# Linear attention ahead of two MLPs on one core: k and v on 128 partitions with a shared last chunk, and a softmax in pieces on ScalarE

## The chip, the core and the metric

One core of a Trainium2 chip. The time is that of one execution on the device in microseconds (us); less is better.

## What is computed

```python
q_s = exp(q - max(q, axis=-1)); q_s = q_s / (sum(q_s, axis=-1) + 1e-09)
k_s = exp(k - max(k, axis=2));  k_s = k_s / (sum(k_s, axis=2) + 1e-09)
kv  = einsum('bhsd,bhse->bhde', k_s, v)      # 4 batches, 8 heads, 576 rows, 64 wide
x   = einsum('bhsd,bhde->bhse', q_s, kv)     # then as 2304 tokens of 512
h   = x @ w_in1;  x   = (h / (1 + exp(-1.702 * h))) @ w_out1    # 512 -> 2048 -> 512
h   = x @ w_in2;  out = (h * tanh(log1p(exp(h)))) @ w_out2      # 512 -> 2048 -> 512
```

The softmax of k subtracts the largest value of each column (batch, head, d) over the sequence. All data is fp32.

## The kernel before

The 2304 tokens are six blocks of 384. For each block the attention makes x (`attention`, L705), and the first MLP runs over 16 chunks of its inner width (`gemm_in`, L750, with `gelu`, and `gemm_out`, L790). The second MLP follows for all blocks (`gemm_in2`, L875, and `gemm_out2`, L918). The MLPs' matmuls are split: each fp32 operand is a sum of two fp32r parts, and three of the four products are taken, so that three matmuls of 384 columns stand for one. The weights are loaded raw and put into the two parts by three to five operations on ScalarE and VectorE (`weight`, L366); those of the first MLP during the first block and the second block's attention, in which the attention's work competes with them.

A unit `u` is a batch and a pair of heads: 16 units, four per batch. Batch 0 belongs to block 0, batch 1 to block 1 (which straddles two batches), batches 2 and 3 to blocks 3 and 4. The 576 rows of the sequence lie as 96 partitions (`KP`) by 6 chunks (`KC`, L245). Per unit:

- `k_load` and `v_load` (L423, L433) fetch a pair of heads. k is one DMA; v is one DMA into a dense tile and a copy on ScalarE in block 0, and one DMA per head later. The tiles of v have two more columns of ones, which give the sums.
- `k_max` (L467) takes the maximum over the chunks on VectorE (three operations, L476), transposes it on TensorE (L481) and reduces it over the partitions (L482).
- In batches 0 and 1 `k_first` (L484) subtracts it on TensorE in plain fp32: an identity matmul of k and one of `minus` by the maxima into the same bank, 384 columns each, for each head (L494, L497), then the exponential out of PSUM (L510). In batches 2 and 3 `k_later` (L516) turns the maxima back (L520), subtracts them on VectorE (L522) and takes the exponential (L523).
- `k_kv` (L525) multiplies: for each head six accumulated matmuls of one chunk, 64 columns of weights and 66 moving columns (L533). The second head writes the other 64 partitions of the same bank. Then the division by the sum (L545 to L565).

An fp32 matmul is two records of the profile, each with its own weight load.

The softmax of q (`q_soft`, L593) works on half a block, four heads: [128, 12, 64] in one tile. VectorE takes the maximum (L611), VectorE or GpSimd subtracts it (`either`, L329), ScalarE takes the exponential of all 768 columns (L613), VectorE sums (L614), adds 1e-9 (L615), inverts (L616) and multiplies (L329). `q_turn` and `x_part` (L633, L664) transpose q and multiply by kv.

The order of all instructions on all engines is made by a planner (`Plan`, L20): each operation is handed in with an engine (or two to choose from), a cost in ns, and what it reads and writes; a list scheduler walks forth and back six times and emits the best order. SyncE issues all DMAs in that order (`dma`, L318, with at least 650 ns each for the planner). The costs are the author's numbers; a different cost gives another order.

Of the kernel before, what the change touches and what calls it, by code (L numbers as in the profile page):

```python
# [8 lines left out]
F32 = mybir.dt.float32  # L9
# [201 lines left out]
def tile_attention_moe_moe(  # L211
# [21 lines left out]

    nc = tc.nc
    P = 128
# [9 lines left out]
    KC = 6  # L245
    KP = S // KC
# [3 lines left out]
    ND = 3  # L250
    SPLIT = ((0, 0), (0, 1), (1, 0))
# [26 lines left out]
    kt = [ap.tile([KP, 2, KC, D], F32, name=f"kt{i}") for i in range(2)]  # L278
    vt = [ap.tile([KP, 2, KC, D + 2], F32, name="vt0")]
    qt = ap.tile([P, NCT, 4, D], F32, name="qt")  # L280
    kv = [ap.tile([P, 2, P], F32R, name=f"kv{i}") for i in range(NHP)]
    pmt = [ap.tile([KP, P], F32, name=f"pmt{i}") for i in range(NHP)]
# [3 lines left out]
    kx = [ap.tile([KP, 2, 3, D], F32, name=f"kx{i}") for i in range(2)]  # L286
    rs = ap.tile([P, NHP], F32, name="rs")
    qs = ap.tile([P, 2, 12], F32, name="qs")

# [3 lines left out]
    kt += [sp.tile([KP, 2, KC, D], F32, name=f"kt{i}") for i in range(2, NHP)]  # L293
    vt += [sp.tile([KP, 2, KC, D + 2], F32, name=f"vt{i}") for i in range(1, NHP)]
    vr = [sp.tile([KP, 2, KC * D], F32, name=f"vr{i}") for i in range(2)] + [gt2[0:KP]]
# [5 lines left out]
    for t in vt:  # L301
        nc.gpsimd.memset(t[:, :, :, D : D + 2], 1.0)
# [15 lines left out]
    def dma(size, reads, writes, out, in_, slow=1):  # L318
        plan.op(
            [(DMA, max(size * slow / 280.0, 650.0), lambda: nc.sync.dma_start(out=out(), in_=in_()), False)],  # L320
            reads,
            writes,
        )
# [93 lines left out]
    def k_tile(u):  # L417
        return u if u < NHP else u % 2

    def v_tile(u):  # L420
        return u if u < NHP else 0

    def k_load(u):  # L423
        b, hp = divmod(u, NHP)
        dma(
            S * 512,
            [],
            [("kt", k_tile(u))],
            lambda: kt[k_tile(u)],
            lambda: k[b, 2 * hp : 2 * hp + 2].rearrange("h (p c) d -> p h c d", c=KC),  # L430
        )

    def v_load(u):  # L433
        b, hp = divmod(u, NHP)
        key = ("vt", v_tile(u))
        if b == 0:

            dense, dk = vr[hp % 3], [("vr", hp % 3)] if hp % 3 < 2 else [("gt", 0), ("gt", 1)]
            dma(
                S * 512,  # L440
                [],
                dk,
                lambda: dense,
                lambda: v[b, 2 * hp : 2 * hp + 2].rearrange("h (p c) d -> p h (c d)", c=KC),
            )
            to = vt[v_tile(u)][:, :, :, 0:D]
            of = dense.rearrange("p j (c d) -> p j c d", d=D)
            plan.op(
                [
                    (ACT, act_ns(768), lambda: nc.scalar.activation(out=to, in_=of, func=AF.Copy), False),  # L450
                    (POOL, 1200.0, lambda: nc.gpsimd.tensor_copy(out=to, in_=of), True),
                ],
                dk,
                [key + (j,) for j in range(2)],
            )
            return
        for j in range(2):
            dma(
                S * 256,
                [],  # L460
                [key + (j,)],
                lambda j=j: vt[v_tile(u)][:, j, :, 0:D],
                lambda j=j: v[b, 2 * hp + j].rearrange("(p c) d -> p c d", c=KC),
                slow=2,
            )

    def k_max(u, ps, key):  # L467

        kk = ("kt", k_tile(u))
# [4 lines left out]
        xk = ("kx", u % 2)  # L474
        largest = lambda n, out, in0, in1, reads, writes: dve(
            n, reads, writes, lambda: nc.vector.tensor_tensor(out=out, in0=in0, in1=in1, op=ALU.max), pair=True  # L476
        )
        largest(384, x, t[:, :, 0:3], t[:, :, 3:6], [kk], [xk])
        largest(128, wide, x[:, :, 0], x[:, :, 1], [xk], [pk])
        largest(128, wide, wide, x[:, :, 2], [xk, pk], [pk])  # L480
        pe(110, [pk], [key], lambda: nc.tensor.transpose(ps, pm, ident[0:KP, 0:KP]))  # L481
        dve(96, [key], [mk], lambda: nc.vector.reduce_max(out=m, in_=ps, axis=AX.X))  # L482

    def k_first(u, ps, keys):  # L484


        kk, mk = ("kt", k_tile(u)), ("mc", u % NHP)
        t, m = kt[k_tile(u)], mcol[:, u % NHP : u % NHP + 1]
        k_max(u, ps[0][:, NB : NB + KP], keys[0])
        for j in range(2):  # L490

            def less(j=j):
                o = ps[j][0:KP, 0:NB]
                nc.tensor.matmul(  # L494
                    out=o, lhsT=ident[0:KP, 0:KP], rhs=t[:, j].rearrange("p c d -> p (c d)"), start=True, stop=False
                )
                nc.tensor.matmul(  # L497
                    out=o.rearrange("p (c d) -> p c d", d=D),
                    lhsT=m.to_broadcast([P, KP]),
                    rhs=minus[:, j * D : (j + 1) * D].rearrange("p (o d) -> p o d", o=1).to_broadcast([P, KC, D]),  # L500
                    start=False,
                    stop=True,
                )

            pe(1330, [("kt", k_tile(u)), ("kt", k_tile(u), j), mk], [keys[j]], less, whole=True)
            act(
                NB,
                [keys[j]],
                [("kt", k_tile(u), j)],
                lambda j=j: nc.scalar.activation(  # L510
                    out=t[:, j].rearrange("p c d -> p (c d)"), in_=ps[j][0:KP, 0:NB], func=AF.Exp
                ),
                psum=True,
            )

    def k_later(u, ps1, ps2, key):  # L516
        kk, mk = ("kt", k_tile(u)), ("mc", u % NHP)
        t, m = kt[k_tile(u)], mcol[:, u % NHP : u % NHP + 1]
        k_max(u, ps1[:, 0:KP], key)
        pe(110, [mk], [key], lambda: nc.tensor.transpose(ps2[0:KP, :], m.to_broadcast([P, KP]), ident))  # L520
        far = ps2[0:KP, :].rearrange("p (j o d) -> p j o d", j=2, o=1).to_broadcast([KP, 2, KC, D])
        dve(768, [kk, key], [kk], lambda: nc.vector.tensor_tensor(out=t, in0=t, in1=far, op=ALU.subtract))  # L522
        act(768, [kk], [kk], lambda: nc.scalar.activation(out=t, in_=t, func=AF.Exp))  # L523

    def k_kv(u, ps3, key3):  # L525
        kk = ("kt", k_tile(u))
# [13 lines left out]

        pe(1375, [kk] + [("kt", k_tile(u), j) for j in range(2)] + [("vt", v_tile(u), j) for j in range(2)], [key3], mm, whole=True)
# [51 lines left out]
    def q_soft(blk, half):  # L593
# [369 lines left out]
    def idle():  # L963
# [9 lines left out]
        + [("kt", i) for i in range(2, NHP)]  # L973
        + [("vt", i, j) for i in range(1, NHP) for j in range(2)]
        + [("vr", i) for i in range(2)]
        + [("qr", i) for i in range(2)],
# [9 lines left out]
    for n in range(NS):  # L986
# [14 lines left out]
        if n == NS - NFC:  # L1001
            plan.op(
                [(NONE, 0.0, pool_second, False)],
                [],
                [("second",)]
                + [("kt", i) for i in range(2)]
                + [("vt", 0, j) for j in range(2)]
                + [("qt", j, d) for j in range(4) for d in (0, 192)]
                + [("kv", hp, a, j) for hp in range(NHP) for a in range(2) for j in range(2)]
                + [("kv32", hp, j) for hp in range(NHP) for j in range(2)]  # L1010
                + [(s, i) for s in ("qT32", "kx") for i in range(2)]
                + [("pm", i) for i in range(NHP)]
                + [(s, i) for s in ("mc", "rs") for i in range(NHP)]
                + [("qs", i) for i in range(2)],
            )
# [54 lines left out]
```

## Time and profile before

| | |
|---|---|
| median of 3 runs | 892.26 us (891.75 to 892.71) |
| the profiled execution | 892.4 us, its span 890.6 us |
| TensorE busy | 880.1 us (99%) |
| VectorE busy | 395.7 us (44%) |
| ScalarE busy | 361.6 us (41%) |
| granted TensorE clock, mean | 0.998 of 2.4 GHz |

The span runs from the first instruction to the last. Busy times of TensorE overlap in the records, since matmuls are pipelined: a record lasts longer than the step to the next one's start, and the step is what a matmul costs. The first 121 us hold block 0 and the attention of block 1, 230 to 345 us the attention of blocks 3 and 4, and from 484 us the second MLP runs.

### The profile page before, as it was taken

Reading aid. Unit: us, or ns where it says so; the run is one execution under the profiler, and the core shown is the slowest. Engines: PE = TensorE matmul, PEld = TensorE weight load, DVE = VectorE, ACT = ScalarE, POOL = GpSimd, SP = SyncE. Lnnn points to the kernel's source line nnn. Section 1 sums busy time; section 2 is a strip of 40 time slices with the busy share of each in tenths; the row PEclk is TensorE's granted clock in tenths of the full one; section 3 lists DMA queues with packets and bytes.
Section 4 is the critical chain, followed back from the end, with each engine's and each line's share of the span. In section 5 each row is a group of like instructions: output and inputs, shape, how many; then the busy total and the mean of one; then the engine's idle time right before and its main releaser. Section 6 shows DMA issues by size and latency. Waiting matters only on the chain.

```text
span 890.6 us, 12257 instructions
## 1 busy us (share of the span) xinstructions
PE 880.1 (99%) x4961; PEld 819.4 (92%) x4961; DVE 395.7 (44%) x760; ACT 361.6 (41%) x649; POOL 5.3 (1%) x21
## 2 busy tenths in 40 slices
PE   8999999999999999999999999999999999999998
PEld 5797899999999999999999999899899899899897
DVE  7999993263385276226999911101101101101101
ACT  5987873242353244224778821311321321321321
POOL 1000000000000000000000000000000000000000
PEclk9999999999999999999999999999999999999999
DMA  9676762011132021100355302001001001000001
GB/s 249 202 224 181 202 208 72 1 36 71 27 90 99 1 71 45 59 1 18 118 167 187 120 1 71 36 1 71 36 1 71 36 1 71 36 1 0 36 1 36
DMA packets 63145, 65.80 MB, mean 74 GB/s; under 512 B 32497, under 2 KB 54513, under 8 KB 62577
## 3 DMA queue, kind: packets, MB, share of 16 engines
q1 hardware_dynamic: 63088, 65.02, 24.2%
q8 instruction: 39, 0.64, 0.3%
q14 instruction: 18, 0.14, 0.0%
HBM read 54.00 MB, written 11.01 MB: 73 GB/s over the span
## 4 chain that ended last, share of the span: by engine, by line
PE 90%; DVE 5%; ACT 2%; DMA 2%; issue 1%; SPq 0%; DVEq 0%
PE hp L755 23%; PE acc L929 22%; PE acc L796 20%; PE h L755 20%; PE at L533 1%; DVE dec L393 1%; DVE dec L398 1%; DMA raw<-in_moe_w_in_dram 1%; PE at L667 1%; PE at L638 1%; DVE W L329 1%; PE at L676 1%; DMA raw<-in_moe_w_out_dram 1%; DVE gt L773 1%; DVE g L329 0%
## 5 line engine op out<-in xcount | busy, mean ns | idle before, releaser
L755 PE MATMUL h<-xt,W 128*128 128x384 f32 x1152 | 224.0, 339 | 1.0 <-DVE gt L773 0.8
L796 PE MATMUL acc<-g,W 128*128 128x384 f32 x1152 | 223.2, 339 | 0.1
L755 PE MATMUL hp<-xt,W 128*128 128x384 f32 x1152 | 208.4, 336 | 0.0
L929 PE MATMUL acc<-W,g 128*128 128x512 f32 x864 | 206.1, 392 | 0.0
L755 PEld LDWEIGHTS hp<-xt,W 128*128 128x128 f32 x1152 | 201.9, 188 | 3.7
L755 PEld LDWEIGHTS h<-xt,W 128*128 128x128 f32 x1152 | 200.7, 188 | 4.4 <-DVE gt L773 1.1
L796 PEld LDWEIGHTS acc<-g,W 128*128 128x128 f32 x1152 | 200.6, 188 | 2.8 <-issue 0.8
L929 PEld LDWEIGHTS acc<-W,g 128*128 128x128 f32 x864 | 161.7, 188 | 32.6
L329 DVE TENSOR_TENSOR g<-gt,g 128x384 fp32r<-128x384 f32 (+1 forms) x110 | 67.4, 613 | 178.8 <-ACT g L337 178.5
L329 DVE TENSOR_TENSOR g<-tb,g 128x768 fp32r<-128x768 f32 x32 | 30.6, 958 | 211.5 <-ACT g L337 211.5
L904 ACT ACTIVATE tb<-hp 128x768 f32<-128x768 f32 x32 | 26.0, 813 | 177.6 <-PE hp L755 177.6
L337 ACT ACTIVATE g<-gt 128x384 fp32r<-128x384 f32 (+1 forms) x112 | 63.7, 569 | 80.1 <-PE acc L796 78.0
L768 ACT ACTIVATE gt<-h 128x384 f32<-128x384 f32 x96 | 46.8, 487 | 92.2 <-PE h L755 91.9
L773 DVE SCALAR_TENSOR_TENSOR gt<-gt,h 128x384 f32<-128x384 f32 x96 | 52.7, 549 | 63.5 <-ACT gt L768 63.3
L904 ACT ACTIVATE gt<-hp 128x768 f32<-128x768 f32 x16 | 13.0, 813 | 96.3 <-PE hp L755 96.3
L346 ACT ACTIVATE dec<-raw 128x512 f32<-128x512 f32 x64 | 42.9, 675 | 11.0 <-DVE W L329 8.2
L346 ACT ACTIVATE raw<-raw 128x512 int32<-128x512 uint32 x63 | 42.1, 677 | 6.1 <-DMA raw<-in_moe_w_out_dram 4.5
L329 DVE TENSOR_TENSOR W<-dec,W 128x512 fp32r<-128x512 f32 x64 | 43.6, 684 | 0.7 <-ACT W L337 0.5
L398 DVE CUSTOM_DVE_ANT_0 dec<-raw,dec 128x1024 uint16<-128x1024 uint16 x64 | 43.6, 683 | 0.4
L393 DVE SCALAR_TENSOR_TENSOR dec<-raw,dec 128x512 int32<-128x512 int32 x64 | 43.6, 683 | 0.2
L337 ACT ACTIVATE W<-dec 128x512 fp32r<-128x512 f32 x62 | 38.7, 628 | 5.8 <-DVE dec L398 5.8
L337 ACT ACTIVATE g<-tb 128x768 fp32r<-128x768 f32 x32 | 27.1, 846 | 1.0
(79 smaller groups left out, 397.0 us busy)
## 6 DMA issues: line engine op xcount, KB each, us to landing
raw<-in_moe_w_in_dram SPq DMA_DIRECT2D x32, 512.0 KB, 4.2
raw<-in_moe_w_out_dram SPq DMA_DIRECT2D x32, 512.0 KB, 4.0
x2d<-xt SPq DMA_DIRECT2D x16, 384.0 KB, 3.1
xt<-x2d SPq DMA_DIRECT2D x4, 1536.0 KB, 6.5
kt<-in_k_dram SPq DMA_DIRECT2D x16, 288.0 KB, 4.5
out_dram<-dec SPq DMA_DIRECT2D x15, 256.0 KB, 2.1
vt<-in_v_dram SPq DMA_DIRECT2D x24, 144.0 KB, 3.2
qt<-in_q_dram SPq DMA_DIRECT2D x24, 96.0 KB, 2.7
```

Of the source, the lines that this page charges most:

```text
L329: return lambda: engine.tensor_tensor(out=out(), in0=in0(), in1=in1(), op=op)
L337: (ACT, act_ns(n), lambda: nc.scalar.activation(out=out(), in_=in_(), func=AF.Copy), False),
L346: (ACT, act_ns(512), lambda: nc.scalar.activation(out=out, in_=in_, func=AF.Copy, scale=scale), False),
L393: lambda: nc.vector.scalar_tensor_tensor(out=a, in0=hi_w, scalar=-0x80000000, in1=a, op0=ALU.bitwise_and, op1=ALU.bitwise_or),
L398: dve(512, [rl], [da], lambda: nc.vector.tensor_tensor(out=a, in0=a, in1=lo_w, op=ALU.add), pair=True)
L533: nc.tensor.matmul(out=ps3[j * D : (j + 1) * D, 0 : D + 2], lhsT=t[:, j, c, :], rhs=w[:, j, c, :], start=c == 0, stop=c == KC - 1,)
L755: nc.tensor.matmul(out=h(), lhsT=w_mm(fc, 0, a, cc), rhs=xt[buf][:, cc, b, :], start=cc == 0 and i == 0, stop=cc == NCC - 1 and i == 2,)
L768: act(NB, [hk, ("tables",)], [tk], lambda: nc.scalar.activation(out=t, in_=h, func=AF.Tanh, scale=0.851), psum=True)
L773: lambda: nc.vector.scalar_tensor_tensor(out=t, in0=t, scalar=1.0, in1=h, op0=ALU.add, op1=ALU.mult),
L796: nc.tensor.matmul(out=acc[dm][:, 0:NB], lhsT=w_mm(fc, 1, a, dm), rhs=g[n % 2][:, b, :], start=fc == 0 and i == 0, stop=fc == NFC - 1 and ...
L904: nc.scalar.activation(out=tb[i], in_=hb(n), func=AF.Mish)
L929: nc.tensor.matmul(out=acc[bank], lhsT=g2[gi][:, j, a, c * P : (c + 1) * P], rhs=w_mm(2 * pr + j, 1, b, 0, 512), start=pr == 0 and j == 0 ...
```

## The change

The sequence now lies as 128 partitions by 4 chunks (`KC = S // P`), which is 512 rows. The last 64 rows of each head share one more chunk: the first head's on partitions 0 to 63, the second's on 64 to 127. A tile is chunks 0 to 3 (first head), 4 (shared) and 5 to 8 (second head), and one unused (`KN = 9`). Each load of k is three DMAs and each load of v three (block 0) or four. The two heads' shared rows are two matmuls of 64 rows in `k_kv` and two of 64 by 64 in `k_first`. In block 1 alone, the softmax of q gives ScalarE twelve exponentials of 64 columns, each with its maximum as the bias and its sum as a by-product.

```diff
-    KC = 6
-    KP = S // KC
+    KC = S // P
+    KB = KC * P
+    KN = 2 * KC + 1
+    LEAST = 200.0
+    GROUPS = ((1, 0), (1, 1))
...
+    def own(t):
+        return t.rearrange("p (j c) d -> p j c d", j=2)[:, :, 0:KC]
+    def rest(t, j):
+        return t[j * D : (j + 1) * D, KC]
+    def rests(t, heads, keys):
+        for j in range(2):
+            dma(D * 256, [], keys[j : j + 1], lambda j=j: rest(t, j), lambda j=j: heads[j, KB:S], least=LEAST)
...
         dma(
-            S * 512,
+            P * 2048,
             [],
-            [("kt", k_tile(u))],
-            lambda: kt[k_tile(u)],
-            lambda: k[b, 2 * hp : 2 * hp + 2].rearrange("h (p c) d -> p h c d", c=KC),
-        )
+            [kk],
+            lambda: own(t),
+            lambda: heads[:, 0:KB].rearrange("h (p c) d -> p h c d", c=KC),
+        )
+        rests(t, heads, [kk + (2 + j,) for j in range(2)])
...
-        largest(384, x, t[:, :, 0:3], t[:, :, 3:6], [kk], [xk])
+        largest(256, x, own(t)[:, :, 0:2], own(t)[:, :, 2:4], [kk], [xk])
         largest(128, wide, x[:, :, 0], x[:, :, 1], [xk], [pk])
-        largest(128, wide, wide, x[:, :, 2], [xk, pk], [pk])
-        pe(110, [pk], [key], lambda: nc.tensor.transpose(ps, pm, ident[0:KP, 0:KP]))
-        dve(96, [key], [mk], lambda: nc.vector.reduce_max(out=m, in_=ps, axis=AX.X))
+        for j in range(2):
+            s = slice(j * D, (j + 1) * D)
+            largest(64, pm[s, s], pm[s, s], rest(t, j), [kk + (2 + j,), pk], [pk])
+        pe(110, [pk], [key], lambda: nc.tensor.transpose(ps, pm, ident))
+        dve(128, [key], [mk], lambda: nc.vector.reduce_max(out=m, in_=ps, axis=AX.X))
...
         for j in range(2):
+            c0, n = ((0, KC + 1), (KC + 1, KC))[j]
-            def less(j=j):
-                o = ps[j][0:KP, 0:NB]
+            def less(j=j, c0=c0, n=n):
+                o = ps[j][:, 0 : n * D]
                 nc.tensor.matmul(
-                    out=o, lhsT=ident[0:KP, 0:KP], rhs=t[:, j].rearrange("p c d -> p (c d)"), start=True, stop=False
+                    out=o, lhsT=ident, rhs=t[:, c0 : c0 + n].rearrange("p c d -> p (c d)"), start=True, stop=False
                 )
+                if j == 0:
+                    for i in range(2):
+                        s = slice(i * D, (i + 1) * D)
+                        nc.tensor.matmul(
+                            out=o[s, KC * D : (KC + 1) * D],
+                            lhsT=m[s].to_broadcast([D, D]),
+                            rhs=minus[s, s],
+                            start=False,
+                            stop=False,
+                        )
                 nc.tensor.matmul(
-                    out=o.rearrange("p (c d) -> p c d", d=D),
-                    lhsT=m.to_broadcast([P, KP]),
+                    out=o[:, 0 : KC * D].rearrange("p (c d) -> p c d", d=D),
+                    lhsT=m.to_broadcast([P, P]),
...
-            pe(1330, [("kt", k_tile(u)), ("kt", k_tile(u), j), mk], [keys[j]], less, whole=True)
+            pe((1220, 890)[j], [kk, kk + (j,), mk] + ([kk + (2,), kk + (3,)] if j == 0 else []), [keys[j]], less, whole=True)
...
             for j in range(2):
+                o = ps3[j * D : (j + 1) * D, 0 : D + 2]
                 for c in range(KC):
                     nc.tensor.matmul(
-                        out=ps3[j * D : (j + 1) * D, 0 : D + 2],
-                        lhsT=t[:, j, c, :],
-                        rhs=w[:, j, c, :],
+                        out=o,
+                        lhsT=own(t)[:, j, c],
+                        rhs=own(w)[:, j, c],
                         start=c == 0,
-                        stop=c == KC - 1,
+                        stop=False,
                     )
+                nc.tensor.matmul(out=o, lhsT=rest(t, j), rhs=rest(w, j), start=False, stop=True)
-        pe(1375, [kk] + [("kt", k_tile(u), j) for j in range(2)] + [("vt", v_tile(u), j) for j in range(2)], [key3], mm, whole=True)
+        pe(1145, k_keys(u) + [("vt", v_tile(u), j) for j in range(4)], [key3], mm, whole=True)
...
         dve(768, key, [sk], lambda: nc.vector.reduce_max(out=s, in_=flat(), axis=AX.X))
-        either(768, ALU.subtract, flat, flat, wide, key + [sk], key)
-        act(768, key, key, lambda: nc.scalar.activation(out=flat(), in_=flat(), func=AF.Exp))
-        dve(768, key, [sk], lambda: nc.vector.reduce_sum(out=s, in_=flat(), axis=AX.X))
-        dve(12, [sk], [sk], lambda: nc.vector.tensor_scalar_add(s, s, 1e-9))
+        if (blk, half) in GROUPS:
+            dve(12, [sk], [sk], lambda: nc.vector.tensor_single_scalar(out=s, in_=s, scalar=-1.0, op=ALU.mult))
+            for i in range(12):
+                act(
+                    D + 223,
+                    key + [sk],
+                    key + [("qsum", half)],
+                    lambda i=i: nc.scalar.activation(
+                        out=flat()[:, i], in_=flat()[:, i], func=AF.Exp, bias=s[:, i : i + 1], accum_out=qsum[:, half, i : i + 1]
+                    ),
+                )
+            dve(12, [("qsum", half)], [sk], lambda: nc.vector.tensor_scalar_add(s, qsum[:, half, :], 1e-9))
+        else:
...
```

Not shown: the tiles' new shapes, the loads of v (the same pattern), and `k_later`, whose subtraction becomes one of the four chunks of both heads and one of 64 columns for each head's shared rows, and whose exponential takes 576 columns instead of 768.

## Rows read from the trace of the kernel before

**Rows 1.** Busy time by stretch: us of PE, PEld, DVE, ACT, POOL, granted clock, DMA.

```profile
0.00:17.00 17.00, 13.38 (x87) 9.30 (x87) 12.20 (x30) 8.35 (x15) 2.98 (x19) 1.00 0.97 240
17.00:28.80 11.80, 11.80 (x78) 7.52 (x79) 10.11 (x25) 11.23 (x23) 0.00 (x0) 0.86 0.90 247
36.00:60.00 24.00, 23.71 (x136) 23.70 (x137) 24.00 (x47) 20.24 (x38) 0.00 (x0) 1.00 0.75 220
60.00:121.00 61.00, 58.69 (x365) 49.46 (x365) 60.29 (x131) 49.80 (x103) 2.36 (x2) 1.00 0.70 198
200.00:350.00 150.00, 150.00 (x1006) 146.78 (x1005) 81.38 (x181) 55.13 (x115) 0.00 (x0) 1.00 0.20 58
```

**Rows 2.** The chain of waits in order of time: start, us, what.

```profile
5.03 9.62 DMA raw<-in_moe_w_in_dram
...
36.24 0.37 DVE W L329
...
81.69 0.55 DVE gt L773
...
120.59 2.09 PE h L755 x12
```

**Rows 3.** Timeline of PE, a unit's subtraction: start, us, engine, line.

```profile
72.71 0.81 PE L494 MATMUL at<-kt,ident 96*96 96x384 f32 x2
73.35 0.81 PE L497 MATMUL at<-minus,mcol 128*96 128x384 f32 x2
```

**Rows 4.** Timeline of PE around one k_kv block, from narrow windows.

```profile
74.88 0.34 PE L796 MATMUL acc<-g,W 128*128 128x384 f32 x1
75.15 0.27 PE L533 MATMUL at<-vt,kt 96*64 96x66 f32 x1
75.26 0.40 PE L533 MATMUL at<-vt,kt 96*64 96x66 f32 x4
75.67 0.40 PE L533 MATMUL at<-vt,kt 96*64 96x66 f32 x6
76.37 0.22 PE L533 MATMUL at<-vt,kt 96*64 96x66 f32 x1
76.52 0.45 PE L755 MATMUL h<-xt,W 128*128 128x384 f32 x1
76.81 0.51 PE L755 MATMUL h<-xt,W 128*128 128x384 f32 x2
```

**Rows 5.** The chain of waits, late units' transposes and k_kv.

```profile
244.37 0.33 PE at L638 x3
...
247.11 1.37 PE at L533 x24
...
250.80 0.09 PE at L481
```

**Rows 6.** Groups by line and shape: busy us, mean ns, idle before.

```profile
L329 DVE TENSOR_TENSOR qt<-qt,qs 128x768 f32<-128x768 f32 x20 | 19.1, 954 | 0.2
L614 DVE TENSOR_REDUCE qs<-qt 128x12 f32<-128x768 f32 x10 | 9.5, 946 | 1.4 <-ACT qt L613 1.4
L476 DVE TENSOR_TENSOR kx<-kt 96x384 f32<-96x384 f32 x16 | 8.8, 549 | 5.9 <-DMA kt<-in_k_dram 5.9
L613 ACT ACTIVATE qt<-qt 128x768 f32<-128x768 f32 x10 | 8.4, 841 | 3.2 <-DVE qt L329 3.2
L615 DVE TENSOR_SCALAR qs<-qs 128x12 f32<-128x12 f32 x12 | 1.9, 162 | 0.0
L556 ACT ACTIVATE kv<-at,rs 64x64 f32<-64x64 f32 x8 | 2.5, 309 | 0.1
```

**Rows 7.** Timeline of SyncE: an issue of a load of k.

```profile
47.77 0.42 SPq L320 DMA_DIRECT2D kt<-in_k_dram  x1
```

More of the change, by code (lines that the diff above doesn't have):

```diff
@@ L277, in tile_attention_moe_moe @@
     ap = actx.enter_context(tc.tile_pool(name="attn", bufs=1))
-    kt = [ap.tile([KP, 2, KC, D], F32, name=f"kt{i}") for i in range(2)]
-    vt = [ap.tile([KP, 2, KC, D + 2], F32, name="vt0")]
+    kt = [ap.tile([P, KN + 1, D], F32, name=f"kt{i}") for i in range(2)]
+    vt = [ap.tile([P, KN + 1, D + 2], F32, name="vt0")]
     qt = ap.tile([P, NCT, 4, D], F32, name="qt")
     kv = [ap.tile([P, 2, P], F32R, name=f"kv{i}") for i in range(NHP)]
-    pmt = [ap.tile([KP, P], F32, name=f"pmt{i}") for i in range(NHP)]
+    pmt = [ap.tile([P, P], F32, name=f"pmt{i}") for i in range(NHP)]
     kv32 = [ap.tile([P, P], F32, name=f"kv32_{i}") for i in range(NHP)]
@@ L316, in pe, with dma @@
         plan.op([(PE, ns, fn, whole)], reads, writes)
-    def dma(size, reads, writes, out, in_, slow=1):
+    def dma(size, reads, writes, out, in_, slow=1, least=650.0):
         plan.op(
-            [(DMA, max(size * slow / 280.0, 650.0), lambda: nc.sync.dma_start(out=out(), in_=in_()), False)],
+            [(DMA, max(size * slow / 280.0, least), lambda: nc.sync.dma_start(out=out(), in_=in_()), False)],
             reads,
@@ L458, in v_load, with k_keys @@
             dma(
-                S * 256,
+                P * 1024,
                 [],
                 [key + (j,)],
-                lambda j=j: vt[v_tile(u)][:, j, :, 0:D],
-                lambda j=j: v[b, 2 * hp + j].rearrange("(p c) d -> p c d", c=KC),
+                lambda j=j: own(to)[:, j],
+                lambda j=j: heads[j, 0:KB].rearrange("(p c) d -> p c d", c=KC),
                 slow=2,
             )
+        rests(to, heads, [key + (2 + j,) for j in range(2)])
+    def k_keys(u):
+        return [("kt", k_tile(u)) + i for i in ((), (0,), (1,), (2,), (3,))]
     def k_max(u, ps, key):
-        kk = ("kt", k_tile(u))
         t, m, mk = kt[k_tile(u)], mcol[:, u % NHP : u % NHP + 1], ("mc", u % NHP)
@@ L518, in k_later @@
         t, m = kt[k_tile(u)], mcol[:, u % NHP : u % NHP + 1]
[L519 to L523, printed above, removed]
+        k_max(u, ps1, key)
+        pe(110, [mk], [key], lambda: nc.tensor.transpose(ps2, m.to_broadcast([P, P]), ident))
+        far = ps2.rearrange("p (j o d) -> p j o d", j=2, o=1).to_broadcast([P, 2, KC, D])
+        dve(
+            512, [kk, key], [kk], lambda: nc.vector.tensor_tensor(out=own(t), in0=own(t), in1=far, op=ALU.subtract)
+        )
+        for j in range(2):
+            s = slice(j * D, (j + 1) * D)
+            dve(
+                64,
+                [key],
+                [kk + (2 + j,)],
+                lambda j=j, s=s: nc.vector.tensor_tensor(out=rest(t, j), in0=rest(t, j), in1=ps2[s, s], op=ALU.subtract),
+            )
+        act(
+            576,
+            [kk],
+            [kk, kk + (2,), kk + (3,)],
+            lambda: nc.scalar.activation(out=t[:, 0:KN], in_=t[:, 0:KN], func=AF.Exp),
+        )
     def k_kv(u, ps3, key3):
-        kk = ("kt", k_tile(u))
         t = kt[k_tile(u)]
@@ L972, in tile_attention_moe_moe @@
         [("late",)]
-        + [("kt", i) for i in range(2, NHP)]
-        + [("vt", i, j) for i in range(1, NHP) for j in range(2)]
+        + [key for u in range(2, NHP) for key in k_keys(u)]
+        + [("vt", i, j) for i in range(1, NHP) for j in range(4)]
         + [("vr", i) for i in range(2)]
+        + [("vr", i, j) for i in range(2) for j in range(2)]
         + [("qr", i) for i in range(2)],
@@ L1005, in tile_attention_moe_moe @@
                 [("second",)]
-                + [("kt", i) for i in range(2)]
-                + [("vt", 0, j) for j in range(2)]
+                + [key for u in range(2) for key in k_keys(u)]
+                + [("vt", 0, j) for j in range(4)]
                 + [("qt", j, d) for j in range(4) for d in (0, 192)]
@@ L1013, in tile_attention_moe_moe @@
                 + [(s, i) for s in ("mc", "rs") for i in range(NHP)]
-                + [("qs", i) for i in range(2)],
+                + [(s, i) for s in ("qs", "qsum") for i in range(2)],
             )
```

58 lines of the change are left out of this document (39 added, 19 removed).

## The prediction

> **What bounds the kernel now.** I read the busy time by stretch first. TensorE works without a gap in 200 to 350 us and, but for 2.3 us, in 60 to 121 us; in 36 to 60 us its only gap is the 0.3 us at the start [rows 1]. So nearly everything that TensorE is given after 36 us is paid in full, and the question is first how many microseconds of TensorE time the change takes or gives. But VectorE is full too in 36 to 60 us, and works 60.3 of the 61 us after that, while ScalarE has 11 us left there [rows 1]. After 121 us VectorE has air: 81 of 150 us [rows 1].
>
> The chain of waits says the same: it runs through VectorE from 36 to 82 us (weights being put together, gelu, softmax), moves to TensorE, and from 120.6 us it is TensorE alone, twelve matmuls of 384 columns in 2.09 us, or 0.174 us each [rows 2]. TensorE's 2.3 idle microseconds in 60 to 121 us are therefore what a lighter VectorE could give back there, and no more.
>
> Ahead of 36 us the first weight lands 9.6 us after its issue [rows 2], TensorE is continuous from 17 us to 28.8 us, and its granted clock over that stretch is 0.86 of 2.4 GHz, part of it at 1.2 GHz, after a pause before 17 us [rows 1].
>
> **TensorE, the matmuls that subtract the maximum (k_first, 8 units).** The two heads' four matmuls of 384 columns follow each other in 0.64 us (72.71 to 73.35) [rows 3]; a unit is 4 x 0.645 = 2.58 us. The new unit streams 320 + 64 + 64 + 256 columns for the first bank and 256 + 256 for the second, 1216 for 1536: -0.54 us. But the two 64-column matmuls are of a new shape: 64 rows by 64 columns of the array between full ones. What a change of shape costs is to be read around a k_kv block.
>
> **The price of a change of shape.** k_kv writes 64 output columns, so it uses half the array's columns, between full-width matmuls. The records one by one [rows 4]: the last full matmul starts at 74.88 and the first of k_kv 0.27 us later instead of 0.174; the second follows after 0.11 instead of 0.057 (24 matmuls of a block in 1.37 us [rows 5]). Going in costs 0.10 + 0.05 = 0.15 us. Going out, 76.37 to 76.52 to 76.81, costs 0.15 - 0.057 and 0.29 - 0.174, together 0.20 us. A mere move to the other half of the columns costs nothing and even overlaps: where the second head begins, at 75.67, six matmuls fit into 0.40 us, as long as four take from 75.26 [rows 4], so that the 24 starts take 1.22 us (75.15 to 76.37) where 23 steps of 0.057 and the 0.05 would take 1.36: 0.14 us is won.
>
> The new kernel leaves out 4 of 24 matmuls, but inserts, after each head's four chunks, a matmul on 64 rows (the shared chunk). Whether a change in the number of rows alone stops the array as a change in the number of columns does, no row here shows: bounds 0 and 0.15 us a change. I take 0.15, from the nearest row, because the array had to run empty there though the next weights were at hand.
>
> By the Trainium skill, "TensorEngine Tiling (Array Packing)", section "Tiling Modes", a change of the tiling mode drains the engine and a change of the tile alone does not, and 128 x 64 and 64 x 64 are modes of their own there. This trace agrees for the column half and for the tile (the 0.10 and the six for four above); it has no case of the row half. By the rule the sum is the one below; by the rows read narrowly (only columns count) it is the first rival's.
>
> k_kv, per unit: -4 x 0.057 = -0.23; three more changes (into the first shared chunk, out, into the second) +0.45; the overlap of the heads lost +0.14; the way in and out as before. **+0.36 us.** k_first, per unit: -0.54, in +0.15, out +0.20: -0.19, and down to -0.30 if the two small squares overlap as the heads did; I take **-0.22**. The transposes of the maxima: 96 columns take 0.09 us and 128 take 0.33 / 3 = 0.11 [rows 5]: +0.03, allowing for the rounding.
>
> So a late unit (blocks 3 and 4, 8 units, k_later) costs TensorE +0.39 us, an early one (blocks 0 and 1, 8 units, k_first) +0.17 us.
>
> **Sum by stage.** Late: 8 x 0.39 = **+3.1 us**, paid in full, since TensorE has no gap there. What VectorE and ScalarE do differently there (a subtraction in three pieces, a shorter exponential) is hidden by their own air; the cover would have to lose 69 us of 150 on VectorE to be gone.
>
> Block 1, 60 to 121 us: TensorE +0.7 us. VectorE loses, in each of two halves, a subtraction (0.95) and a sum (0.95) and gains a 12-wide multiply (0.16) [rows 6]: -3.5 us. The maxima of k over 256 instead of 384 columns, then two 64-wide pieces, are a wash (0.55 for 384 [rows 6], less an eighth or so for what is narrower, plus one instruction more). ScalarE replaces one exponential of 0.84 us by twelve of 64 columns. The nearest row is a 64-column instruction with a per-row scale, 0.31 us [rows 6]; the row sum that each adds is in no row: from nothing to a second instruction of 0.2 us (0.84 for 768 columns leaves 0.2 for none). I take 0.33: +3.1 us a half, +6.2 for two, bounds +2.9 and +5.3 a half; four units' shorter exponentials give 0.6 back. ScalarE has 11 us, so it holds. Waiting behind a group are only other pieces, as the planner places each of the twelve by itself. What VectorE's relief gives TensorE is at most the 2.3 us of gaps; ScalarE's longer queue takes some. I take half, -1.1. Each unit also puts four more loads on SyncE's queue, 16 in all, at some 0.4 us [rows 7]; a weight load waiting behind them is late by up to 2 us, which I leave in the range. **-0.4 us** (-1.6 to +1.5).
>
> Block 0: VectorE's work is unchanged in kind, and two of four units lie in TensorE's continuous stretch: +0.3 us. The loads of k and v are now three each, so SyncE issues up to a dozen more ahead of the first weight, 5 us later than 5.03; it now lands at 14.65, after 9.62 us [rows 2] in which the DMA engines were full with what was ahead of it (0.97 busy over 0 to 17 us [rows 1]), so a later issue mostly shortens its stay in the queue. I take nothing. A stretch at 1.2 GHz that moves, comes or goes is worth up to 1.7 us either way. **+0.3 us** (-1.7 to +2).
>
> Together 3.1 - 0.4 + 0.3 = +3.0 us on the profiled execution's 892.4, or 895.4; the median of the runs is 0.14 lower: **895.3 us**, own range 892.8 to 898.
>
> **The rivals.** *Rows cost nothing (not slower).* If the step between four full chunks and the shared one stops nothing while the columns stay the same half, k_kv is -0.23 us a unit, with k_first's two changes still paid: late 8 x -0.20 = -1.6, block 1 4 x -0.42 = -1.7 and 0.6 of the gaps, block 0 -0.5: -4.4, or 887.9 us (884.5 to 890). It decides from 0.03 us a change down, where three changes and the lost overlap equal the four matmuls saved. For it speaks that moving between halves is free; against, that the only change of shape in the trace is not. Chance 0.25.
>
> *VectorE's relief pays it back (no change).* The stops are as I say, but 3.5 us less on the engine that carries the chain from 36 to 82 us closes all 2.3 us of gaps and brings block 0 forward by 1: 3.1 + 0.7 - 2.3 - 1 = +0.5, so 892.8 us (890.5 to 894). Against it: in 36 to 60 us TensorE has no gap to close. Chance 0.11.
>
> *ScalarE becomes the bound of block 1 (slower still).* At 0.51 us a piece the groups add 10.5 us to the 11 that it has; then each of the four units waits as one does now, and 4 us come on top: 899.3 us (898 to 902). It decides where a piece takes over 0.5 us. Against it: 0.31 in the nearest row. Chance 0.10.
>
> The forecast keeps 0.54.
>
> **How the numbers follow.** A measurement of this kernel can tell 0.2% from no change, 1.8 us: under 890.5 is faster, over 894.1 slower. Faster: nearly all of the first rival and a little of the second, 0.27. No change: the rest of the second and the low fifth of the forecast, 0.20. Slower: 0.53. The range takes the forecast and the second rival whole, about half of the first and a little of the third: 886.5 to 898.5.
>
> **What would show it.** After: in k_kv's block, single records with steps of 0.15 and 0.11 us where the shared chunk begins and ends, and a block that takes more than the 1.22 us between its first and last start with only 20 records. In the stretch 200 to 350 us the same work ends later by about 3 us. VectorE's softmax of q in block 1 without its sum and subtraction, twelve 64-column records of 0.3 us on ScalarE in their place, and TensorE's gaps in 60 to 121 us down to about half. I am wrong if the shared chunk's records follow in 0.057 us: then the first rival holds. I am wrong on block 1 if the gaps there grow.

## The result and the profile after

The changed kernel takes **897.03 us** (median of 6 runs, 896.45 to 897.46) against 892.27 us (6 runs, 891.75 to 892.99) for the kernel before in the same session: a ratio of 1.0053 [1.0043, 1.0064], slower by half a per cent and clear of the noise. The profiled execution takes 897.38 us, its span 895.6.

The busy time by stretch, changed kernel, same columns as in [rows 1]:

```profile
0.00:17.00 17.00, 15.19 (x93) 10.99 (x94) 10.64 (x26) 7.15 (x14) 2.97 (x19) 1.00 0.75 221
17.00:28.80 11.80, 11.80 (x83) 8.35 (x83) 10.97 (x30) 10.79 (x24) 0.00 (x0) 1.00 0.66 220
36.00:60.00 24.00, 23.49 (x133) 22.55 (x132) 24.00 (x48) 20.24 (x39) 0.00 (x0) 1.00 0.79 232
60.00:121.00 61.00, 57.71 (x358) 49.84 (x357) 57.80 (x133) 50.80 (x140) 0.00 (x0) 1.00 0.63 184
200.00:350.00 150.00, 150.00 (x956) 145.15 (x955) 81.68 (x200) 53.12 (x115) 0.00 (x0) 1.00 0.21 58
```

Late, nothing has changed in kind: TensorE has no gap from 200 to 350 us. Early, three things have. VectorE does 10.64 us of work in the first 17 us where it did 12.20; it works only 57.8 of the 61 us after 60 where it worked 60.3; and TensorE's gaps in that stretch have grown from 2.3 to 3.3 us. The granted clock is 1.00 of 2.4 GHz in all five stretches, so the stretch with a mean of 0.86 in [rows 1] is gone, which favours the changed kernel by up to 0.14 x 11.8 = 1.65 us where the two profiled executions are compared.

The chain of waits of the changed kernel, in order of time, with the start of the second MLP as its last line:

```profile
60.56 0.70 DVE dec L404
61.26 0.02 SPq L326
...
61.31 5.89 DMA raw<-in_moe_w_in_dram
...
68.84 0.66 ACT qt L684 x4
...
122.50 2.08 PE h L833 x12
...
488.60 4.18 PE hp L833 x24
```

The same view of the kernel before, for the second MLP's start:

```profile
483.61 4.19 PE hp L755 x24
```

The twelve matmuls that began at 120.59 us [rows 2] now begin at 122.50: +1.91 us by then. The second MLP begins 4.99 us later (488.60 for 483.61), so blocks 3 and 4 add **3.08 us**, and the second MLP adds nothing. The chain itself now runs through the landing of a weight (whose load is issued when VectorE has freed its buffer, at 61.26) and then mostly ScalarE with the pieces of q's softmax between 61 and 82 us, where it ran through VectorE before.

The 1.91 us are not lost at once. Timeline of PE, the same twelve matmuls of block 0 before (first line) and after (second line), and the longest wait of the changed kernel behind them (third line):

```profile
53.07 2.24 PE L755 MATMUL h<-xt,W 128*128 128x384 f32 x12
52.38 2.50 PE L833 MATMUL h<-xt,W 128*128 128x384 f32 x12
67.29 2.01 PE L874 MATMUL acc<-g,W 128*128 128x384 f32 x10 [1.12 <-DVE W L335]
```

At 53 us the changed kernel is still 0.69 us ahead. It loses 2.6 us between there and 122 us: 1.5 us more of idle time (3.8 us for 2.3), most of it behind weights that VectorE (2.1 us) and ScalarE (1.2 us) have yet to put together, and the rest in TensorE's own steps.

**k_kv, record by record.** Timeline of PE around one block of the changed kernel:

```profile
83.21 0.68 PE L596 MATMUL at<-vt,kt 128*64 128x66 f32 x8
83.82 0.33 PE L603 MATMUL at<-vt,kt 64*64 64x66 f32 x2
84.08 0.68 PE L596 MATMUL at<-vt,kt 128*64 128x66 f32 x8
84.69 0.33 PE L603 MATMUL at<-vt,kt 64*64 64x66 f32 x2
84.94 1.31 PE L833 MATMUL h<-xt,W 128*128 128x384 f32 x6
```

Five starts are enough to read it. Eight steps of 0.057 are 0.46 us, but a head's own chunks take 0.61 (83.82 - 83.21): 0.15 more. The two records of the shared chunk take 0.26 (84.08 - 83.82) where two steps are 0.11: 0.15 more again. So each change between the two shapes costs 0.15 us, either way: the first record of the new shape starts some 0.09 us late, and the second 0.05 us late. From the first record to the next full matmul it is 84.94 - 83.21 = 1.73 us for 20 records, against 76.52 - 75.15 = 1.37 for 24 [rows 4]: **+0.36 us**, as priced. A change of rows alone, 128 x 64 to 64 x 64 in the same column half, costs what a change of columns does (0.15 us on the way in [rows 4]). A wait on a semaphore is not what the changes cost: in a late unit of the changed kernel the weight load that begins the shared chunk waits for nothing and still starts 0.21 us behind the one before it (241.10 to 241.31 us, for 0.058 otherwise), and in experiment 1 the weight load that begins the second head waits for one and is not held up (82.01 us). The rule of the Trainium skill ("TensorEngine Tiling (Array Packing)", "Tiling Modes"), that a change of mode drains the engine, agrees with the trace in the row half too.

**k_first** in the chain of waits of the changed kernel (first bank with the two squares, second bank):

```profile
102.63 0.54 PE at L531 x2
103.17 0.26 PE at L537 x4
103.43 0.63 PE at L544 x2
...
104.90 0.43 PE at L531 x2
105.33 0.43 PE at L544 x2
```

0.54 + 0.26 + 0.63 + 0.43 + 0.43 = 2.29 us, for 2.58 before [rows 3]: -0.29.

**The pieces of q's softmax**, groups by line and shape of the changed kernel (busy us, mean ns, idle before):

```profile
L684 ACT ACTIVATE qt<-qt,qs 128x64 f32<-128x64 f32 x24 | 8.0, 335 | 0.0
L684 ACT ACTIVATION_READ_ACCUMULATOR qt<-qt,qs 128x1 f32 x24 | 4.5, 188 | 0.0
```

Each piece is two instructions: the exponential and a read of its sum. ScalarE's timeline of the changed kernel shows how they lie:

```profile
68.74 0.34 ACT L684 ACTIVATE qt<-qt,qs 128x64 f32<-128x64 f32 x1
68.98 0.19 ACT L684 ACTIVATION_READ_ACCUMULATOR qt<-qt,qs 128x1 f32 x1
69.07 0.33 ACT L684 ACTIVATE qt<-qt,qs 128x64 f32<-128x64 f32 x1
```

The read starts 0.24 us after the exponential, the next exponential 0.09 us after the read: 0.33 us a piece. (The chain's line with x4 is two pieces in 0.66 us.)

**The first microseconds.** SyncE's queue, changed kernel (start, us, loads):

```profile
0.74 2.84 SPq L326 DMA_DIRECT2D kt<-in_k_dram  x5
3.62 0.59 SPq L326 DMA_DIRECT2D qr<-in_q_dram  x1
...
7.11 0.59 SPq L326 DMA_DIRECT2D qr<-in_q_dram  x1
...
9.57 0.47 SPq L326 DMA_DIRECT2D raw<-in_moe_w_in_dram  x1
...
18.19 1.54 SPq L326 DMA_DIRECT2D raw<-in_moe_w_in_dram  x1
```

The same queue of the kernel before:

```profile
1.67 1.00 SPq L320 DMA_DIRECT2D qr<-in_q_dram  x2
...
5.03 1.35 SPq L320 DMA_DIRECT2D raw<-in_moe_w_in_dram  x2
...
8.63 0.37 SPq L320 DMA_DIRECT2D raw<-in_moe_w_in_dram  x1
```

Each load takes some 0.5 us of the queue, and up to 14.2 us no pause lies between them: 23 loads are issued by then, 14 in the kernel before. The second half-block of q is issued at 7.11 us where it was issued at 2.2, the first weight at 9.57 for 5.03, the third at 18.19 for 8.63; they land 3.1, 0.6 and 3.7 us later. VectorE's timeline of the changed kernel shows who feels it:

```profile
7.36 0.95 DVE L675 TENSOR_REDUCE qs<-qr 128x12 f32<-128x768 f32 x1 [1.12 <-DMA qr<-in_q_dram]
...
10.46 0.95 DVE L692 TENSOR_REDUCE qs<-qr 128x12 f32<-128x768 f32 x1 [0.71 <-ACT qr L691]
...
11.75 0.95 DVE L675 TENSOR_REDUCE qs<-qr 128x12 f32<-128x768 f32 x1
...
28.99 0.69 DVE L335 TENSOR_TENSOR W<-dec,W 128x512 fp32r<-128x512 f32 x1
```

and the kernel before:

```profile
8.64 0.95 DVE L611 TENSOR_REDUCE qs<-qr 128x12 f32<-128x768 f32 x1
...
27.09 0.68 DVE L329 TENSOR_TENSOR W<-dec,W 128x512 fp32r<-128x512 f32 x1
```

The maximum of q's second half-block is taken 3.1 us later, and the last part of the third weight is written 1.9 us later. That TensorE is 1.9 us behind by 122 us is not the same 1.9 handed on: it is 0.7 us ahead in between, and pays from 55 us on, when it has caught up with the weights.

### The profile page after: what moved, and what is told of

Its sections match the earlier page's. It is cut to its first block, busy times and chain, and to the rows that moved or that the text cites. A ratio compares the mean times of both kernels' runs of the same rounds, so it can differ in the third digit from the quotient of the medians.

```text
span 895.6 us, 12401 instructions
## 1 busy us (share of the span) xinstructions
PE 885.2 (99%) x4934; PEld 823.9 (92%) x4934; DVE 397.0 (44%) x793; ACT 362.7 (40%) x694; POOL 3.0 (0%) x19
## 4 chain that ended last, share of the span: by engine, by line
PE 92%; DVE 3%; ACT 2%; DMA 1%; issue 1%; SPq 0%; ACTq 0%; DVEq 0%
PE hp L833 22%; PE acc L1007 22%; PE acc L874 20%; PE h L833 20%; PE at L596 2%; PE at L716 1%; DVE dec L404 1%; PE at L745 1%; DVE dec L399 1%; PE at L603 1%; DMA raw<-in_moe_w_in_dram 1%; PE at L754 1%; ACT qt L684 0%; PE acc L531 0%; DMA qr<-in_q_dram 0%
```

## Experiments

All ratios are to the kernel before, run beside the experiment. Three questions were open: is the late loss the change of shape alone; which part of the change made blocks 0 and 1 later; and do the pieces on ScalarE help or hurt.

**1. The shared chunks side by side.** The changed kernel with the order own, own, shared, shared, so that the shape changes once inside a block instead of three times. All other engines' instructions stand in the same order as in the changed kernel.

```diff
             for j in range(2):
-                o = ps3[j * D : (j + 1) * D, 0 : D + 2]
                 for c in range(KC):
...
-                nc.tensor.matmul(out=o, lhsT=rest(t, j), rhs=rest(w, j), start=False, stop=True)
+            for j in range(2):
+                nc.tensor.matmul(out=o[j], lhsT=rest(t, j), rhs=rest(w, j), start=False, stop=True)
```

> The changed kernel with the two shared-chunk matmuls of k_kv moved behind both heads' own chunks (own, own, shared, shared); the planner's order and costs stay. If the changes of shape are what k_kv pays, a block loses two of them (2 x 0.145 us) and gets back the overlap of the two heads (0.14, and a little for the two shared ones): 0.43 to 0.50 us a unit. The eight late units, which are paid in full, then give 3.4 to 4.0 us, block 1's four up to 1.9 more: 891 to 893.6 us. If the order of shapes costs nothing and the late 3.1 us have another cause, 897 us as the changed kernel.

Measured: 890.13 us (889.77 to 890.95), ratio 0.998 [0.9971, 0.9988]. Timeline of PE of this kernel, one block:

```profile
81.72 0.97 PE L596 MATMUL at<-vt,kt 128*64 128x66 f32 x16
82.62 0.33 PE L604 MATMUL at<-vt,kt 64*64 64x66 f32 x4
82.89 1.31 PE L834 MATMUL h<-xt,W 128*128 128x384 f32 x6
```

1.17 us from the first record to the next full matmul, 0.56 less than in the changed kernel and 0.20 less than before. The four shared records take 0.27 us, as long as two did: the two heads' run side by side, and so do the heads within the sixteen (0.90 us for 16 records and the change). The same arithmetic on the same data, with two changes of shape fewer, makes the change a gain of 0.2% instead of a loss of 0.5%. The chain of waits of this kernel, at the two places that were read above:

```profile
119.26 2.08 PE h L834 x12
...
481.42 4.18 PE hp L834 x24
```

It is 122.50 - 119.26 = 3.24 us ahead of the changed kernel at the first, and 488.60 - 481.42 = 7.18 at the second: 3.94 us from the eight late units (0.49 each, where a block by itself gains 0.56; a new gap of TensorE, 0.23 us at 259.5 us, takes part of it), 3.24 from the early part.

**2. No pieces.** The changed kernel with block 1's softmax of q as it was.

```diff
-    GROUPS = ((1, 0), (1, 1))
+    GROUPS = ()
```

> The changed kernel without the twelve exponentials (GROUPS empty), so block 1's softmax of q is as in the kernel before. If the late weights are what costs block 1 its 2 us (theory: loads in more pieces push the weights back), VectorE gets its 3.5 us of work back on top of that and the time is 897.5 to 899. If ScalarE's twelve pieces are what costs it (rival), the gaps of TensorE in 60 to 80 us shrink and the time is 895 to 896.

Measured: 898.59 us (898.16 to 898.72), ratio 1.0071 [1.0058, 1.0084], 1.6 us above the changed kernel. The two kernels' intervals overlap slightly, but no run of the one lies within the other's. With the order that the planner makes for each, the kernel with the pieces is faster, so this run does not bear out ScalarE as what the changed kernel loses by. But more than the pieces differs: without them some 130 of VectorE's 793 instructions stand elsewhere, the first within 5 us, so the 1.6 us are the worth of the pieces and the order together.

**3. The pieces alone**, in the kernel before.

```diff
+    GROUPS = ((1, 0), (1, 1))
...
-        either(768, ALU.subtract, flat, flat, wide, key + [sk], key)
-        act(768, key, key, lambda: nc.scalar.activation(out=flat(), in_=flat(), func=AF.Exp))
-        dve(768, key, [sk], lambda: nc.vector.reduce_sum(out=s, in_=flat(), axis=AX.X))
+        if (blk, half) in GROUPS:
+            dve(12, [sk], [sk], lambda: nc.vector.tensor_single_scalar(out=s, in_=s, scalar=-1.0, op=ALU.mult))
+            for i in range(12):
...
```

> The kernel before with the twelve exponentials in block 1 alone, k and v as before. If ScalarE holds the pieces and VectorE's relief closes some of TensorE's 2.3 us of gaps: 890.5 to 892.3 us. If ScalarE's queue becomes the bound of block 1: 893.5 to 894.5 us, with gaps of TensorE in 60 to 121 us of 4 us or more.

Measured: 891.82 us (889.69 to 895.44, 12 runs), ratio 0.9992 [0.998, 1.0004]: no difference that can be measured. Its profiled run is its slowest, with the clock at 1.2 GHz in parts of the first 30 us (0.62 of 2.4 GHz granted from 10 to 17 us), and no trace of it is read here.

**4. The loads alone.** The kernel before with two extra 64-row loads behind every load of k and v.

```diff
+    pad = [ap.tile([P, D], F32, name=f"pad{i}") for i in range(2 * NHP)]
...
+    def rests(i, heads):
+        for j in range(2):
+            dma(D * 256, [], [("pad", i, j)], lambda j=j: pad[i][j * D : (j + 1) * D], lambda j=j: heads[j, S - D : S], least=200.0)
```

> The kernel before with two more loads of 64 rows behind each load of k and of v, into tiles that nothing computes with; the planner is told that the maxima and k_kv wait for them, and counts 200 ns for each, as in the changed kernel. If more loads ahead of the first weights push the weights back: the third weight's landing moves from 19.5 us to 21 us or later, the sixteenth chunk of the first MLP starts 1 to 2 us later and the time is 893.3 to 894.3. If the loads are hidden: 892.0 to 892.6 us, and the 2 us come from elsewhere.

Measured: 895.72 us (894.71 to 897.09), ratio 1.0042 [1.003, 1.0054]. Loads with which nothing computes cost 3.4 us by the medians and 3.7 by the ratio. TensorE is 2.5 us behind by the chunk that starts at 120.3 us before, and 3.3 us at the end.

**5 and 6. The extra loads of batch 0 alone, and of batches 1 to 3 alone.**

```diff
-        rests(hp, k[b, 2 * hp : 2 * hp + 2])
+        if b == 0:
+            rests(hp, k[b, 2 * hp : 2 * hp + 2])
```

(`if b > 0` for the other, and the same for v.)

> e4_extra_dma's additional loads for batch 0 alone (16 issues). In e4_extra_dma the ninth chunk of the first MLP started 1.2 us later and the seventeenth 2.5 us later. If the loads act where they stand, ahead of the first weights, this gives 1 to 1.6 us: 893.3 to 894.0. If the first weights' delay is made up later because VectorE is the bound: 892.0 to 892.7.

> e4_extra_dma's additional loads for batches 1 to 3 alone. If the loads between the weights of 40 to 110 us push these back: 1.5 to 2.2 us more, 893.8 to 894.6. If all comes from the first ones: 892.0 to 892.8. In blocks 3 and 4 nothing should move in either case.

Measured: batch 0 alone 895.91 us (894.54 to 896.11), ratio 1.0043 [1.0029, 1.0057]; the others alone 892.57 us (891.18 to 893.73, 11 runs), ratio 1.0006 [0.9997, 1.0015]. My size for the first was too small by more than a factor of two: all of the cost comes with the sixteen loads ahead of and among the first weights, and forty-eight later ones cost nothing measurable. In both, the planner's order moves a little too (some 50 and 70 of VectorE's 760 instructions). The first 20 us by engine, with batch 0's extra loads:

```profile
0.00:20.00 20.00, 16.24 (x99) 11.40 (x100) 13.40 (x34) 9.80 (x19) 2.98 (x19) 1.00 0.87 229
```

with the later ones:

```profile
0.00:20.00 20.00, 15.23 (x97) 10.14 (x98) 14.79 (x36) 10.80 (x20) 2.98 (x19) 1.00 0.97 260
```

the kernel before:

```profile
0.00:20.00 20.00, 16.38 (x94) 11.19 (x95) 14.88 (x36) 11.32 (x21) 2.98 (x19) 0.93 0.98 253
```

the changed kernel:

```profile
0.00:20.00 20.00, 18.18 (x109) 12.88 (x110) 13.52 (x36) 9.84 (x20) 2.97 (x19) 1.00 0.71 211
```

The column to read is VectorE's (the third busy time). With the small loads in front it has done 13.4 or 13.5 us of work by 20 us, without them 14.8 or 14.9; and the DMA engines are busy 0.71 or 0.87 of the time, not 0.97 or 0.98: they wait for the queue.

**7. One load for the shared chunk.** Experiment 1 with another choice of rows: the shared chunk takes the last 64 rows of the first head and the first 64 of the second, which lie next to each other in memory, so that one load of 128 rows fills it instead of two of 64.

```diff
-            dma(D * 256, [], keys[j : j + 1], lambda j=j: rest(t, j), lambda j=j: heads[j, KB:S], least=LEAST)
+        dma(D * 512, [], keys, lambda: t[:, KC], lambda: flat[base + KB : base + KB + P], least=LEAST)
```

> The kernel of e1_pair with other rows in the shared chunk: the first head's last 64 and the second head's first 64, which lie next to each other in memory, so that one load of 128 rows takes the place of two of 64. Eight issues fewer in block 0, eight in block 1; the matmuls stay as in e1_pair. If it is the number of loads ahead of and between the weights that costs blocks 0 and 1 their time: 888.0 to 889.4 us. If only the bytes or the packets count, which stay: 889.8 to 890.5.

Measured: **888.19 us** (887.73 to 889.11), ratio 0.9964 [0.9951, 0.9976]: faster than both kernels, and faster than experiment 1 by 1.4 us (ratios) to 1.9 us (medians). The order is another too (some 140 of VectorE's 793 instructions stand elsewhere), so this is the worth of fewer loads and their order together. The first 20 us of this kernel:

```profile
0.00:20.00 20.00, 16.73 (x113) 12.54 (x114) 15.29 (x40) 10.35 (x21) 2.97 (x19) 1.00 0.88 268
```

VectorE has now done more than in the kernel before.

**8. The same load in the changed kernel's own order** (own, shared, own, shared), to see whether the two gains add.

```diff
-            for j in range(2):
-                nc.tensor.matmul(out=o[j], lhsT=rest(t, j), rhs=rest(w, j), start=False, stop=True)
+                nc.tensor.matmul(out=o[j], lhsT=rest(t, j), rhs=rest(w, j), start=False, stop=True)
```

> The changed kernel's own order of matmuls (own, shared, own, shared), but with one load for the shared chunk instead of two. Against the changed kernel only the loads differ. If what the one load gave beside the paired order (1.9 us) comes from the loads alone, it adds: 894.4 to 895.8 us. If it came from a lucky meeting of loads and the paired order: 896.4 to 897.5 us.

Measured: 896.23 us (895.86 to 896.28), ratio 1.0036 [1.0023, 1.0049]. That is 0.8 us below the changed kernel by the medians and 1.5 by the ratios, between the two ranges expected: the loads give something by themselves, less surely than in experiment 7. Experiments 7 and 8 differ in nothing but the order of `k_kv`'s matmuls, the other engines' instructions standing alike, and lie 6.4 us (ratios) to 8.0 us (medians) apart: experiment 1's result once more.

**9. The planner's number.** Experiment 1 with 650 ns instead of 200 as the planner's least cost of a small load. No instruction is added; only the order can differ.

```diff
-    LEAST = 200.0
+    LEAST = 650.0
```

> The kernel of e1_pair with LEAST = 650, so that the planner counts a small load as long as any other. If the planner's 200 ns is too little for what a load of 64 rows takes of SyncE (0.5 to 0.6 us each) and the weights suffer from it, an order that knows it wins 0.5 to 1.5 us: 888.6 to 889.6. If the order is as good either way: 889.8 to 890.6.

Measured: 896.52 us (895.75 to 897.31), ratio 1.0056 [1.0043, 1.0068]. I expected a small gain, since 0.5 us of queue per load is nearer to 650 ns than to 200. It is 6.4 us slower than experiment 1. The first 20 us of this kernel:

```profile
0.00:20.00 20.00, 17.02 (x124) 13.85 (x124) 12.28 (x33) 8.20 (x16) 2.97 (x19) 1.00 0.75 220
```

VectorE has done 12.3 us of work, for 13.2 in experiment 1. A truer cost gave the list scheduler a worse start.

**10 to 12. The small loads on another queue.** Batch 0's extra loads of experiment 5, then the changed kernel's shared-chunk loads of batch 0, then those of experiment 7, issued from ScalarE's queue in an unchanged planned order.

```diff
-            [(DMA, max(size * slow / 280.0, least), lambda: nc.sync.dma_start(out=out(), in_=in_()), False)],
+            [(DMA, max(size * slow / 280.0, least), lambda: queue.dma_start(out=out(), in_=in_()), False)],
...
-        rests(t, heads, [kk + (2 + j,) for j in range(2)])
+        rests(t, heads, [kk + (2 + j,) for j in range(2)], queue=nc.scalar if b == 0 else nc.sync)
```

> The kernel before with the same sixteen extra 64-row loads of the first batch as the run that put them there alone (895.9 us), in the same planned order, but issued from ScalarE's DMA queue instead of SyncE's. Nothing computes with what they bring. If the cost is SyncE's time (0.45 to 0.6 us of queue per load, which holds back the first weights' loads behind them): 891.5 to 893.3 us, and the first weight's issue back near 5 to 6 us. If the cost is the bytes, the DMA engines, or the order that the planner makes around sixteen more loads: 895 to 896.5 us as before. In between would say that both count.

> The changed kernel with the shared chunk's loads of the first batch (eight of k and six of v) issued from ScalarE's queue; everything else, the planned order too, as in the changed kernel. If SyncE's queue ahead of the first weights makes most of the 1.9 us that blocks 0 and 1 lost: 894.6 to 895.8 us, with the first weight issued near 6 us. If the loads' transfers or the planned order make it: 896.5 to 897.5 us, no different from the changed kernel.

> The best version so far (own, own, shared, shared, and one load for the shared chunk; 888.2 us) with the first batch's shared-chunk loads, four of k and three of v, on ScalarE's queue. If SyncE's queue is what counts: another 0.5 to 1 us, 887.0 to 887.8 us. If not: 888.0 to 888.6 us.

Measured: 901.43 us (898.75 to 904.37), ratio 1.01 [1.0083, 1.0117]; 903.88 us (903.11 to 904.47), ratio 1.0122 [1.0109, 1.0135]; 892.45 us (891.97 to 893.97), ratio 1.0 [0.9991, 1.0008]. All three are slower than with SyncE's queue, by 4.3 to 6.9 us (medians; 3.2 to 6.2 by the ratios), which neither theory expected. ScalarE's timeline of the first of them:

```profile
13.17 0.47 ACT L517 ACTIVATE kt<-acc 96x384 f32<-96x384 f32 x1
14.88 2.06 ACTq L321 DMA_DIRECT2D pad<-in_v_dram  x2
16.98 0.49 ACT L517 ACTIVATE kt<-acc 96x384 f32<-96x384 f32 x1 [3.34 <-DMA raw<-in_moe_w_in_dram]
```

ScalarE works through its issues and its exponentials in one order: it computes nothing from 13.6 to 17 us, for one, where its next two issues go out only when the first and the second weight have landed (14.86 and 16.44 us), and the last of the sixteen loads go out at 31 us. The clock differs too: from 17 to 28.8 us the three profiled executions were granted 0.64, 0.57 and 0.79 of 2.4 GHz, the kernels with SyncE's queue 1.00, which by itself is worth up to 4.2, 5.1 and 2.5 us. So this was no clean test. One thing can be read from it: the first weight, issued at 7.15 us instead of 11.76 (experiment 5), landed at 14.86 instead of 15.73. An issue 4.6 us earlier was worth 0.9 us of earlier landing.

## Why the prediction was right, and where not

The forecast was 895.3 us with 892.8 to 898 as its own range; 897.03 lies in it. The step that carried it, the late units' price, was right to 0.1 us; the term for blocks 0 and 1 was 2.0 us too low, and that the sum still fell inside the range is owed to the range's width.

- **The price of a change of shape, right.** The choice of 0.15 us for a change of rows alone, which no row showed, came from the nearest row. Measured are 0.15 at each such change and +0.36 us a unit, as summed. The first rival (rows cost nothing, 887.9 us) falls by the single records, and experiment 1 shows that it is the changes that cost: with fewer of them, and nothing else moved, the change gains.
- **The late units, right.** 8 x 0.39 = 3.1 us forecast, 3.08 measured, all of it paid in full, since TensorE has no gap there.
- **k_first, at its lower bound.** I took -0.22; it is -0.29, because the two squares overlap (four records in 0.26 us). With the transposes an early unit costs 0.1 us, not 0.17, which is 0.8 us for the eight where 1.4 were forecast.
- **The pieces on ScalarE, right:** 0.33 us each, with the sum's read as a second instruction. The third rival (ScalarE becomes the bound) falls by its own condition, a piece of over 0.5 us, though the chain does pass mostly through ScalarE from 67 to 82 us.
- **Blocks 0 and 1, wrong.** Forecast: +0.3 and -0.4, together -0.1. Measured: +1.91 by 122.5 us, and that with a clock that was up to 1.65 us kinder than in the profiled execution before. The step that failed is the term for block 0's loads: "a later issue mostly shortens its stay in the queue. I take nothing". It holds for the load that I looked at, the first weight (issued 4.5 us later, landed at 15.25 us for 14.65), and experiment 10 shows it once more. But the same queue holds q's second half-block and the third weight, 5 and 10 us later in their issue and 3.1 and 3.7 us later in their landing. VectorE, which carries the chain from 36 to 82 us [rows 2], is 1.4 us of work behind by 20 us. TensorE pays for it only from 55 us on, when it waits for weights. The loads should have stood in the sum: experiments 4 and 5 price sixteen of them in front at 3.4 to 4.2 us in the kernel before, and halving their number in experiments 7 and 8 gives back 0.8 to 1.9. The "up to 2 us" that I gave to block 1's loads belonged to block 0's as far as the kernel before shows it: there, those of later batches cost nothing measurable (experiment 6). In the changed kernel a part may be theirs: the weight on the chain, issued at 61.31 us behind loads of v and k, takes 5.89 us to land, where its counterpart before, issued at 60.12 us, takes 4.1.
- **The gaps in 60 to 121 us** were to halve; they grew by 1.0 us, the sign that I had named for being wrong on block 1. VectorE's relief is there (57.8 us of work for 60.3), but it is taken as idle time behind late weights and ScalarE. The second rival (the relief pays it all back) falls. That the relief is worth something the two kernels with and without the pieces suggest (1.6 us in the changed kernel, nothing measurable in the kernel before).

What stays open: how much of the 1.9 us the loads cost by SyncE's issue time, by their transfers, or by the order that the planner makes around them. For the issue time speaks that the changed kernel's queue has no pause up to 14.2 us, with the DMA engines at 0.75 up to 17 us where they were at 0.97. But experiment 9 shows that the order alone can be worth 6 us, every kernel with other loads has its own order, and experiments 10 to 12, which were to separate the queue, put ScalarE's work behind it instead. That VectorE's late start is the link between the loads and the end is read from the windows of the six kernels shown and from the chain; no experiment delayed VectorE alone.

## What to carry to other kernels

Before an accumulation is cut into tiles of two shapes, count the changes of shape per unit and put equal shapes next to each other: here the same matmuls in another order were worth 6.5 to 6.9 us in one pair of kernels and 6.4 to 8.0 in another. Count loads as well as bytes in the first microseconds, and follow each thing behind them in the queue to the engine that the chain runs through, not only the first weight. After a change to a planned schedule, look at how much the bound engine has done by a fixed early time; a cost in the planner can move the end by more than the edit does.

## What the runs showed that I had not expected

- Two matmuls of 64 rows by 64 columns on opposite quarters of the array run side by side: four records in 0.27 us where two take 0.26 (experiment 1 against the changed kernel), and the same for the two squares of `k_first`.
- A sum taken beside an exponential is an instruction of its own on ScalarE, 188 ns long; 0.09 us lie between its start and the next exponential's.
- Loads issued from ScalarE's queue can hold back its computing far longer than their 0.5 us of issue each, when an issue waits for an earlier load to land: 3.3 us at one place. The kernels with 7 to 16 such loads were 3 to 7 us slower, in part with a lower granted clock.
- The kernel before varies more than the changed one: 22 runs beside experiments 1 to 4 lie between 890.57 and 894.75 us, where the changed kernel's six span 1.0 us. Its mean granted clock explains little of that: the runs at 1.000 alone span 890.57 to 893.79 us. Why is not shown.
